# An S5 layer gated with a feed-forward layer on one core: a recurrence at every second token, one-pass silu, and a new order of the work

## The chip, the core and the metric

One core of a Trainium2 chip runs the program. The metric is device time in microseconds (us): the median of several executions of the compiled program. Most executions agree within 1.5% with the fastest of their kernel and are called fast here. A few were slower: some of the kernel before (up to 356.99 us against 349.31), one of e7 (352.45) and one of e10 (313.36, at a granted clock of 0.825 where the others had 0.85). A ratio compares fast runs alone. Where a run is compared with another, both were timed in the same rounds or set against the same kernel before (e9 to e12 ran on another chip than e1 to e8; the kernel before took 350.84 us there).

Engines in the profile: PE is TensorE's matmuls, PEld its weight loads, DVE is VectorE, ACT is ScalarE, POOL is GpSimd, SP is SyncE, which only issues DMAs here. A name with a small q (SPq, ACTq) is the sequencer of that engine. L345 is line 345 of the kernel that the profile is of, so the numbers differ from kernel to kernel.

## The reference, cut to what matters

```python
S, D, F = 2048, 448, 1792                     # tokens, model width, feed-forward width
g  = sigmoid((x * gate_w).sum(-1))            # one gate per token
dt = exp(log_dt); lam = exp(dt * Lambda)      # 448 complex lanes
B_bar = ((lam - 1) / Lambda)[:, None] * B
Bu = x @ B_bar.T                              # complex input
h_t = lam * h_{t-1} + Bu_t                    # 2048 steps, independent per lane
a  = 2 * real(h @ C.T) + x * Dskip
b  = silu(x @ w1) @ w2
out = g * a + (1 - g) * b                     # [1, 2048, 448] bf16
```

The recurrence over 2048 tokens is complex. Both kernels turn it into two real scans per lane: the input is rotated back by the lane's angle, `v_t = u_t * exp(-i*t*theta)`; then real and imaginary part each follow `g_t = r * g_{t-1} + v_t` with a real `r`, which is one scan instruction of VectorE; the result is rotated forward again. The rotations need a table of cosines and sines.

## The kernel before

A helper records every operation with the names of the buffers that it reads and writes, and turns these into semaphore waits. Each engine is given its own instructions as one list, in the order in which the program recorded them, and a wait in that list holds up what stands behind it.

The feed-forward tile. Silu takes two ScalarE passes and a VectorE product:

```python
def ffn1_tile(tc, fb):                        # 4 matmuls of 512 columns; the 4th uses 64 rows only
    T.op("pe", mm, reads=["w1", "xt"], writes=[f"ps{bank}"])
    T.op("act", ... activation(sig[slot], ps[:, bank, 0:512], AF.Sigmoid))            # L331
    T.op("act", ... activation(aT[:, fb, :], ps[:, bank, 0:512], AF.Copy))            # L342
    T.op("dve", ... tensor_tensor(aT[:, fb, :], aT[:, fb, :], sig[slot], ALU.mult))   # L345
```

The recurrence: 4 groups of lanes times 4 chunks of 512 tokens make 16 rounds.

```python
def s5_bu(pb, tc):                            # 2 x 4 matmuls, 2 evictions by ScalarE (L385)
    ...
def s5_rot_scan(pb, tc):                      # all VectorE
    p1 = ur*COS; p2 = ui*SIN; vr = p1+p2      # bf16, L398 to L402
    p1 = ui*COS; p2 = ur*SIN; vi = p1-p2      # bf16, L404 to L408
    ... carry in from the chunk before (4 small operations) ...
    gr = scan(R, vr); gi = scan(R, vi)        # float32 out, L437, L439
    q1 = gr*COS; q2 = gi*SIN; Hre = q1-q2     # L452 to L456
    q1 = gr*SIN; q2 = gi*COS; Him = q1+q2     # L458 to L462
```

The order, with feed-forward tiles strewn between the rounds, and the DMA names (all parts of x have one name, so that each DMA waits for the one before):

```python
for eb in range(4):
    T.dma("sp", ... dma_start_transpose(xt[eb][:, :], x2[:, c0:c0 + 128]), g_x, writes=["xt"])
... parameter arithmetic on 128 x 448 rows, B_bar on 4 x 128 x 448, tables; ffn1 tiles between ...
for step in range(4):
    for tcc in range(NTC):
        s5_bu(step, tcc)
        ... up to 7 ffn1 tiles or 2 ffn2 blocks ...
        s5_rot_scan(step, tcc)
for tb in range(12, 16): ffn2_block(tb)
for tb in range(NTB):    final_block(tb, tb)  # 8 matmuls, gate, one ACT pass, three DVE passes, store
```

## Time and profile before

| | before |
|---|---|
| time, median of 4 | 351.14 us (349.35 to 353.99) |
| span of the profiled run | 348.3 us |
| PE / DVE / ACT busy | 197.8 / 228.5 / 133.2 us |
| mean granted clock of TensorE | 0.794 |
| chain that ended last | DVE 54%, ACT 18%, PE 12%, DMA 9% |

The page of the kernel before. The first lines are busy time, share of the span and number of instructions of each engine; the rows of digits cut the span into 40 slices of 8.7 us, where a digit is the busy share in tenths, and PEclk is the granted clock of TensorE in tenths of full speed; the last line is the chain of waits followed back from the last instruction.

```profile
span 348.3 us, 2549 instructions
PE 197.8 (57%) x774; PEld 66.2 (19%) x784; DVE 228.5 (66%) x458; ACT 133.2 (38%) x258; POOL 1.6 (0%) x11
...
PE   0002722501760599810484995575994665899994
DVE  0000269981574699999675799484899484927776
PEclk9999955655555559985596999696999696899998
...
DVE 54%; ACT 18%; PE 12%; DMA 9%; issue 4%; ACTq 2%; DVEq 0%
```

No engine is full. The granted clock of TensorE is 0.50 in much of the time in which it has little to do (0.50 from 80 to 130 us) and 1.00 in the dense stretch from 310 to 340 us; in the first 40 us, in which TensorE is busy for 7.5 us only, the view lists 1.00. The windows view (busy time and count for each engine in a stretch, then granted clock, DMA share and GB/s) shows three stages: head, rounds, output.

```profile
33.00:116.00 83.00, 30.75 (x71) 6.54 (x72) 48.32 (x95) 43.10 (x74) 0.00 (x0) 0.59 0.15 38
116.00:296.00 180.00, 121.57 (x439) 39.51 (x448) 144.17 (x296) 69.31 (x129) 0.00 (x0) 0.81 0.00 1
296.00:348.00 52.00, 44.82 (x248) 19.55 (x248) 36.02 (x67) 18.33 (x53) 0.00 (x0) 0.94 0.22 65
```

The waits view (who waited for what: us in total, times, longest) and the groups by form (busy us, mean ns of one, idle time just before) of the kernel before:

```profile
DVE t L345 <- ACT t L342: 82.9, 40, 36.1
...
L331 ACT ACTIVATE t<-ps 128x512 bf16<-128x512 f32 x56 | 33.6, 599 | 93.1 <-DVE t L345 75.2 <-PE ps L325 17.9
L437 DVE TENSOR_TENSOR_SCAN t<-t 128x512 f32<-128x512 f32 x12 | 15.2, 1264 | 0.0
L452 DVE TENSOR_TENSOR t<-t 128x512 bf16<-128x512 f32 x12 | 8.0, 667 | 0.0
L404 DVE TENSOR_TENSOR t<-t 128x512 bf16<-128x512 bf16 x12 | 5.1, 425 | 0.4
```

The first line is the silu hand-over: VectorE stood 82.9 us in front of silu's product, 36.1 of it once at the start, when the first tile's inputs had not landed yet. The second is the other side: ScalarE stood 75.2 us in front of the sigmoid until VectorE had done a product, because VectorE came to it only after the scans that stood before it in its own order. One full-width round of rotations and scans costs VectorE 6 x 0.42 + 2 x 1.25 + 4 x 0.68 + 2 x 0.42 = 8.6 us.

### The profile page before, as it was taken

Reading aid. Unit: us, or ns where it says so; the run is one execution under the profiler, and the core shown is the slowest. Engines: PE = TensorE matmul, PEld = TensorE weight load, DVE = VectorE, ACT = ScalarE, POOL = GpSimd, SP = SyncE. Lnnn points to the kernel's source line nnn. Section 1 sums busy time; section 2 is a strip of 40 time slices with the busy share of each in tenths; the row PEclk is TensorE's granted clock in tenths of the full one; section 3 lists DMA queues with packets and bytes.
Section 4 is the critical chain, followed back from the end, with each engine's and each line's share of the span. In section 5 each row is a group of like instructions: output and inputs, shape, how many; then the busy total and the mean of one; then the engine's idle time right before and its main releaser. Section 6 shows DMA issues by size and latency. Waiting matters only on the chain.

```text
span 348.3 us, 2549 instructions
## 1 busy us (share of the span) xinstructions
PE 197.8 (57%) x774; PEld 66.2 (19%) x784; DVE 228.5 (66%) x458; ACT 133.2 (38%) x258; POOL 1.6 (0%) x11
## 2 busy tenths in 40 slices
PE   0002722501760599810484995575994665899994
PEld 0000100100110124300020441121441111444331
DVE  0000269981574699999675799484899484927776
ACT  0003880319624622400363433454432545124443
POOL 1000000000000000000000000000000000000000
PEclk9999955655555559985596999696999696899998
DMA  6877421100000100000000000000000000003332
GB/s 100 147 192 204 125 53 40 26 2 0 0 0 17 24 0 0 0 1 0 0 0 2 0 2 0 1 1 0 0 2 0 0 0 0 0 2 105 109 104 68
DMA packets 23661, 11.55 MB, mean 33 GB/s; under 512 B 16672, under 2 KB 23200, under 8 KB 23648
## 3 DMA queue, kind: packets, MB, share of 16 engines
q1 hardware_dynamic: 18304, 5.77, 7.2%
q10 hardware_dynamic: 5344, 5.62, 6.5%
q8 instruction: 6, 0.10, 0.1%
q14 instruction: 7, 0.06, 0.1%
HBM read 5.62 MB, written 1.84 MB: 21 GB/s over the span
## 4 chain that ended last, share of the span: by engine, by line
DVE 54%; ACT 18%; PE 12%; DMA 9%; issue 4%; ACTq 2%; DVEq 0%
PE ps L325 8%; DVE t L437 5%; DVE t L439 5%; DMA t<-in_B_w_dram 5%; ACT t L342 4%; PE ps L357 4%; DVE t L505 3%; DVE t L458 3%; ACT t L331 3%; DVE t L460 3%; DVE t L454 3%; DVE t L452 3%; DVE t L546 2%; ACT t L499 2%; DVE t L456 2%
## 5 line engine op out<-in xcount | busy, mean ns | idle before, releaser
L325 PE MATMUL ps<-t 128*128 128x512 bf16 (+1 forms) x218 | 77.9, 469 | 105.4 <-ACT t L342 81.0
L345 DVE TENSOR_TENSOR t<-t 128x512 bf16<-128x512 bf16 x56 | 23.1, 424 | 83.0 <-ACT t L342 82.9
L331 ACT ACTIVATE t<-ps 128x512 bf16<-128x512 f32 x56 | 33.6, 599 | 93.1 <-DVE t L345 75.2
L379 PE MATMUL ps<-t 128*128 128x512 bf16 (+1 forms) x124 | 42.8, 458 | 16.3 <-ACT t L385 15.7
L325 PEld LDWEIGHTS ps<-t 128*128 128x128 bf16 x224 | 18.9, 104 | 163.6 <-issue 143.8
L357 PE MATMUL ps<-t 128*128 128x448 bf16 x224 | 46.0, 366 | 1.6 <-DVE t L345 1.6
L342 ACT ACTIVATE t<-ps 128x512 bf16<-128x512 f32 x56 | 33.5, 598 | 0.0
L357 PEld LDWEIGHTS ps<-t 128*128 128x128 bf16 x224 | 22.1, 101 | 24.4 <-issue 3.6
L385 ACT ACTIVATE t<-ps 128x512 bf16<-128x512 f32 (+1 forms) x32 | 18.7, 602 | 16.5 <-PE ps L379 11.5
L476 PE MATMUL ps<-t 128*128 128x448 bf16 x64 | 22.8, 357 | 1.5 <-ACT t L499 1.5
L363 ACT ACTIVATE t<-ps 128x448 bf16<-128x448 f32 x16 | 8.7, 543 | 37.7 <-PE ps L357 37.7
L479 PE MATMUL ps<-t 128*128 128x448 bf16 x64 | 22.5, 352 | 0.0
L437 DVE TENSOR_TENSOR_SCAN t<-t 128x512 f32<-128x512 f32 (+1 forms) x16 | 20.2, 1265 | 0.0
L379 PEld LDWEIGHTS ps<-t 128*128 128x128 bf16 (+1 forms) x128 | 11.1, 103 | 47.8 <-issue 43.7
L439 DVE TENSOR_TENSOR_SCAN t<-t 128x512 f32<-128x512 f32 (+1 forms) x16 | 19.9, 1247 | 0.0
L505 DVE SCALAR_TENSOR_TENSOR t<-t 128x448 f32<-128x448 bf16 x16 | 10.9, 684 | 12.8 <-ACT t L499 12.2
L546 DVE TENSOR_TENSOR t<-t 128x448 f32<-128x448 f32 (+1 forms) x17 | 10.0, 617 | 5.3 <-ACT t L560 3.2
L538 ACT ACT_TABLE_LOAD x1 | 1.3, 1283 | 30.5 <-issue 30.5
L534 PE MATMUL ps<-t 1*128 1x1 bf16 x16 | 0.6, 161 | 20.6 <-DMA t<-in_gate_w_dram 20.6
L458 DVE TENSOR_TENSOR t<-t 128x512 bf16<-128x512 f32 (+1 forms) x16 | 11.1, 691 | 0.6
L508 DVE SCALAR_TENSOR_TENSOR t<-t 128x448 bf16<-128x448 bf16 x16 | 11.0, 685 | 0.6
L454 DVE TENSOR_TENSOR t<-t 128x512 bf16<-128x512 f32 (+1 forms) x16 | 11.0, 689 | 0.0
(88 smaller groups left out, 199.7 us busy)
## 6 DMA issues: line engine op xcount, KB each, us to landing
t<-in_A_x_dram ACTq DMA_DIRECT2D x16, 112.0 KB, 2.0
out_dram<-t SPq DMA_DIRECT2D x16, 112.0 KB, 1.8
t<-in_B_w_dram ACTq DMA_DIRECT2D x1, 1568.0 KB, 7.7
t<-in_B_w_dram ACTq DMA_DIRECT2D x3, 448.0 KB, 3.7
t<-in_B_w_dram ACTq DMA_DIRECT2D x1, 224.0 KB, 3.6
t<-in_A_log_dt_dram ACTq DMA_DIRECT2D x1, 112.0 KB, 3.9
t<-in_A_Lambda_re_dram ACTq DMA_DIRECT2D x1, 112.0 KB, 4.2
t<-in_A_Lambda_im_dram ACTq DMA_DIRECT2D x1, 112.0 KB, 4.4
```

What stands on the lines that cost most here:

```text
L325: ins = pe.matmul(ps[:, bank, 0:512], w1s[i][p0:p0 + K, fb * 128:(fb + 1) * 128], xt[i][p0:p0 + K, t0:t0 + 512], start=(i == 0), stop=(i = ...
L331: T.op("act", lambda eng: eng.activation(sig[slot][:, :], ps[:, bank, 0:512], AF.Sigmoid), reads=[f"ps{bank}"], writes=[f"sig{slot}"])
L342: T.op("act", lambda eng: eng.activation(aT[:, fb, :], ps[:, bank, 0:512], AF.Copy), reads=[f"ps{bank}"], writes=[f"aT{fb}"])
L345: lambda eng: eng.tensor_tensor(aT[:, fb, :], aT[:, fb, :], sig[slot][:, :], ALU.mult),
L357: ins = pe.matmul(ps[:, bank, 0:D_MOD], aT[:, fb, tl:tl + 128], w2s[:, fb, :], start=(fb == 0), stop=(fb == NFB - 1))
L379: ins = pe.matmul(ps[0:q0 + M, bank, 0:512], Bb[p0:p0 + K, i, lane0mm:lane0mm + q0 + M], xt[i][p0:p0 + K, t0:t0 + 512], start=(i == 0), st ...
L437: T.op("dve", lambda eng: eng.tensor_tensor_scan(gr[q0:q0 + M, :], Rbc, vr[q0:q0 + M, :], init_r, ALU.mult, ALU.add), reads=[f"vr{s}", "cf ...
L439: T.op("dve", lambda eng: eng.tensor_tensor_scan(gi[q0:q0 + M, :], Rbc, vi[q0:q0 + M, :], init_i, ALU.mult, ALU.add), reads=[f"vi{s}", "cf ...
L454: T.op(Epool, lambda eng: eng.tensor_tensor(qp2[q0:q0 + M, :], gi[q0:q0 + M, :], SIN, ALU.mult), reads=[f"gi{s}", f"SIN{pb}"], writes=[nqp2])
L458: T.op(Edve, lambda eng: eng.tensor_tensor(qd1[q0:q0 + M, :], gr[q0:q0 + M, :], SIN, ALU.mult), reads=[f"gr{s}", f"SIN{pb}"], writes=[nqd1])
L476: ins = pe.matmul(ps[:, bank, 0:D_MOD], Hre[q0:q0 + M, pb, t0:t0 + 128], C2T[q0:q0 + M, pb, :], start=first, stop=False)
L479: ins = pe.matmul(ps[:, bank, 0:D_MOD], Him[q0:q0 + M, pb, t0:t0 + 128], Ci2T[q0:q0 + M, pb, :], start=False, stop=(pb == 3))
```

## The change

The intent is to halve the sequential work and to take everything that is not a matmul off the long chain.

- **Recurrence at every second token.** With `h_{2k+1} = lam^2 * h_{2k-1} + (lam*B x_{2k} + B x_{2k+1})` only odd states are scanned: 1024 steps. The input matmul takes two tokens at once (7 blocks of 128 rows). An even token's output is `C lam h_{2k-1} + (C B + D) x_{2k}`, where the dense `K0 = C B + D` is built once and costs four matmuls per tile.
- **Scaling in C.** The factor `(lam-1)/Lambda` goes into C, so raw B is transposed and parameters are 128 x 4 columns rather than 128 x 448 rows. Real and imaginary part of the last 64 lanes share one full tile.
- **Silu in one ScalarE pass**; the gate on VectorE with an accumulating product; only DMA transposes; separate names for separate DMAs; tables of 1024 steps.
- **A new order.** All "side" work (tables, C, gate) is pumped between the first 28 feed-forward tiles; then input matmuls and scans, then the rest of the feed-forward layer, then the output tiles.

The diff, cut to its core (the whole replaces most of the file; cuts are marked `...`):

```diff
-            T.op("act", lambda eng: eng.activation(sig[slot][:, :], ps[:, bank, 0:512], AF.Sigmoid), ...)
-                T.op("act", lambda eng: eng.activation(aT[:, fb, :], ps[:, bank, 0:512], AF.Copy), ...)
-                     lambda eng: eng.tensor_tensor(aT[:, fb, :], aT[:, fb, :], sig[slot][:, :], ALU.mult),
+            T.op("act", lambda e: e.activation(a[:, fb, :], ps[:, bank, :], AF.Silu), ...)
...
+        def bu(m, h):                            # m: real/imaginary tile, h: half of the 1024 pairs
+                for j in range(7):
+                    ins = pe.matmul(ps[:, bank, :], LT[:, m, j, :], XT[:, j, h * 512:(h + 1) * 512], ...)
+            T.op("act", lambda e: e.activation(HS[:, m, 8 + h * 512:8 + (h + 1) * 512], ps[:, bank, :], AF.Copy), ...)
...
-            T.op("dve", lambda eng: eng.tensor_tensor_scan(gr[q0:q0 + M, :], Rbc, vr[q0:q0 + M, :], init_r, ...
+                T.op("dve", lambda e: e.tensor_tensor_scan(G[:, c, :], rb, Q1[:, c, :], 0.0, ...   # 1024 long
...
+        def ytile(kt, odd):
+                for m in range(8):
+                    ins = pe.matmul(ps[:, bank, 0:D], HS[:, m, o0:o0 + 128], C[:, m, :], ...)
+                ... odd: 4 small diagonal matmuls; even: 4 x matmul(XT[:, j], KT[:, j, :]) ...
+            T.op("dve", ... scalar_tensor_tensor(o, ps[:, bank, 0:D], GT[:, 1, tile:tile + 1], bs(tile), ...
...
+        side = chain(side_params(), side_tables(0), side_coef(), side_diag(), side_C(True),
+                     side_tables(1), side_gate(), side_tables(2), side_tables(3), side_C(False))
+        for _ in range(2):
+            next(side)
+        for c in range(2):
+            for fb in range(NFB):
+                ffn1(c, fb)
+                pump()
+        for pt in range(3):
+            ... bu(2*pt, h), bu(2*pt+1, h), pump(2) ...; scan(pt) ...
+        ... bu(6, h), bu(7, h); rest of side; scan(3); k0; ffn2(0); ffn1(2); ffn2(1); ffn1(3); ffn2(2) ...
+        for q in range(4):
+            ffn2(3, q); ytile(q, 0); ytile(q, 1); store(q)      # then the last eight tiles
```

## The prediction

> **What bounds the kernel now.** No single engine: PE 57% busy, DVE 66%, ACT 38% (page, part 1), but the chain that ended last is 54% DVE, 18% ACT, 12% PE, 9% DMA. Three stages show in the windows view. (1) 0–116 us: input DMAs wait for each other (chain: log_dt, Lambda_re, Lambda_im, Dskip, then w1 until 32.9 us), then parameter arithmetic on 128x448 rows (0.62 us an op, reciprocal 2.95) and cos/sin tables. (2) 116–296 us: 16 rotate-and-scan rounds, DVE 97% busy in them; one costs 6x0.42 + 2x1.25 + 4x0.68 + 2x0.42 = 8.6 us; between rounds DVE stands behind the silu hand-over (PE, two ACT passes, one DVE multiply per tile). (3) 296–348 us: one ffn2 group and 16 output tiles at 2.2 us, paced by DVE/ACT; full TensorE clock.
>
> **What changes.** Scan length halves. Sizes of 1024 estimated from the 512 durations (bf16 product 0.42 to 0.69, scan 1.25 to 2.3, float product 0.68 to 1.22): three pairs at 15.1 us plus 6.9 us for the packed last one, 52 us of DVE for 138. Silu becomes one ACT pass with no DVE multiply (56x0.60 ACT and 56x0.42 DVE gone). ACT u-evictions fall from 32 to 16. Output tiles need no ACT, one DVE op. Row arithmetic becomes 128x4 (0.16 us an op). PE hardly shrinks: matmuls of 512 columns go from 352 to 336, of about 448 from 352 to about 400. K=64 pieces vanish. Added on DVE ahead of the first scan: B combinations (7), C combinations (16) at about 1.05 us (0.39 + 0.68), four tables at 2.7, coefficients 5, 16 gate products at 0.68.
>
> **Where the critical path goes.** From the instruction order:
> - About 17–20 us: inputs (transposes no longer serialised) and parameters; then DVE runs all side work in order. It also gates ACT: silu tiles sit behind table and tanh instructions in ACT's order, so the first 28 ffn1 tiles are paced by DVE. B combinations to 25, table 0 to 28, coefficients/diagonals 34, odd C 43, table 1 46, gate about 62 (two buffers, reloads about 2 us each), tables 2 and 3 share a buffer with ACT, 77; last silus to about 83 us. TensorE is sparse here and at half clock (0.50 in such windows now).
> - Then PE never waits for the scans (they end about 146 us, the output tiles start about 185). Its remaining order, at the cadence of dense full-clock stretches (0.19 us per 448; 0.215 per 512 estimated by columns): input matmuls 24, K0 6, ffn2 43, ffn1 24, output tiles 33 = 130 us, plus 4 for warm-up and boundaries. Last eviction and store 3 us.
>
> Span about 83+134+3 = 220; the measured time stands 3 us above the span: **223 us**, range 206 to 243. Chances: faster by over 2% 0.98, same 0.01, slower 0.01.
>
> The Trainium skill ("TensorE: Matmul & The Clock Gate", What's actually happening) says the array clock is halved until activity lasts some microseconds; this trace agrees (0.50 in sparse windows, 1.00 at 310–340 us). It matters twice: the DVE-paced head stays slow, the tail runs full.
>
> **What would show it.** Right: PE over 90% busy at clock near 1.0 in the last 60%, chain nearly all PE there; first 80 us DVE-led with PE under 5 tenths; scans ending some 40 us before the first output tile; DVE total near 135–150 us, ACT near 85. Wrong: PE waiting on scans; output tiles paced by evictions through two banks; ACT over 100.
>
> **What would make it wrong.** Transposes from on-chip memory, or about 12 MB of input at the 160–200 GB/s seen early, delaying the gate loads past 50 us (slower by 5–20); table loads of 1.28 us at every silu/sine switch; a cheaper gate phase (faster by up to 10); reduced clock or slower weight loads at odd offsets in the dense tail.

## The result, and the profile after

| | before | after |
|---|---|---|
| time, median of 4 | 351.14 us | 215.06 us (214.43 to 217.03) |
| ratio of the fast runs | | 0.6131 (0.608 to 0.6182) |
| span of the profiled run | 348.3 us | 213.8 us |
| PE / DVE / ACT busy | 197.8 / 228.5 / 133.2 us | 163.9 / 114.1 / 71.3 us |
| chain that ended last | DVE 54%, ACT 18%, PE 12% | PE 62%, DVE 15%, DMA 11% |

A ratio here sets the fast runs of one kernel against those of the other in the same rounds, so it isn't quite the ratio of the medians quoted. Forecast 223 (range 206 to 243), measured 215.06. The page after:

```profile
span 213.8 us, 2064 instructions
PE 163.9 (77%) x784; PEld 77.2 (36%) x792; DVE 114.1 (53%) x212; ACT 71.3 (33%) x112; POOL 7.3 (3%) x16
...
PE   0550009939703349999999999999999999999994
DVE  0439999903567696499999999700000021213332
PEclk9997556975985557999999999999999999999999
...
PE 62%; DVE 15%; DMA 11%; SPq 7%; ACT 3%; issue 1%; DVEq 0%
```

A slice is 5.3 us here. PE is at 9 from the sixteenth slice on, the clock from the seventeenth: one dense stretch. The windows view cuts it at the end of the head (82 us) and at the end of the scans (138 us):

```profile
14.00:82.00 68.00, 30.03 (x97) 11.17 (x99) 49.79 (x128) 29.22 (x42) 0.00 (x0) 0.68 0.54 133
82.00:138.00 56.00, 55.79 (x268) 26.54 (x271) 50.62 (x51) 23.13 (x40) 0.00 (x0) 0.99 0.00 1
138.00:211.00 73.00, 72.56 (x398) 37.49 (x398) 10.55 (x16) 15.60 (x26) 0.00 (x0) 1.00 0.06 23
```

TensorE is busy 128.4 of 129 us after the head. In the head it is busy 30 of 68 us. The waits view says what it stood for, and the chain (start, us, what) says what stood behind that:

```profile
PE ps L493 <- ACT AT L498: 37.9, 5, 17.6
...
DVE JK L457 <- DMA OT<-in_A_x_dram: 11.9, 5, 8.3
```

```profile
41.92 9.41 DMA OT<-in_A_x_dram
51.35 0.65 DVE JK L457 x2
...
75.27 0.95 ACT G L384
76.25 1.15 ACT COS L385
77.39 0.49 ACT AT L498
77.89 0.05 issue
77.93 3.59 PE ps L493 x8
81.53 7.12 PE ps L528 x29
```

L498 is silu. In these long waits it did not wait for its own matmuls: it stood in ScalarE's order behind tables (L382 to L385) and the tanh from which the gate's sigmoid is made, which wait for VectorE, which for 8.3 us waited for the first gate tile. Two groups by form answer to those of before, the scan and the product with a float32 operand, now on 1024 elements:

```profile
L564 DVE TENSOR_TENSOR_SCAN G<-P,Q 128x1024 f32<-128x1024 f32 x7 | 15.7, 2278 | 0.0
L561 DVE TENSOR_TENSOR Q<-G,COS 128x1024 bf16<-128x1024 f32 x6 | 7.3, 1210 | 0.0
L561 DVE TENSOR_TENSOR Q<-HS,COS 128x1024 bf16<-128x1024 bf16 x7 | 4.8, 685 | 3.9 <-ACT HS L532 3.9
```

The scan and the float32 product nearly double from 512 to 1024 elements (1264 to 2278 ns, 667 to 1210 ns), and the bf16 product goes from 425 to 685 ns.

So the change turned a kernel in which VectorE and ScalarE pass work to and fro for most of 348 us into a head of 82 us with the same disease, and a tail of 129 us that is nothing but matmuls. That raises the question that the experiments answer: which parts of the change earned the 136 us?

### The profile page after: what moved, and what is told of

Its sections match the earlier page's. It is cut to its first block, busy times and chain, and to the rows that moved or that the text cites. A ratio compares the mean times of both kernels' runs of the same rounds, so it can differ in the third digit from the quotient of the medians.

```text
span 213.8 us, 2064 instructions
## 1 busy us (share of the span) xinstructions
PE 163.9 (77%) x784; PEld 77.2 (36%) x792; DVE 114.1 (53%) x212; ACT 71.3 (33%) x112; POOL 7.3 (3%) x16
## 4 chain that ended last, share of the span: by engine, by line
PE 62%; DVE 15%; DMA 11%; SPq 7%; ACT 3%; issue 1%; DVEq 0%
PE ps L511 20%; PE ps L493 13%; PE ps L528 12%; PE ps L610 11%; DMA OT<-in_A_x_dram 8%; SPq L208 4%; SPq L205 3%; DVE JK L457 3%; PE ps L621 3%; DMA Y<-in_A_B_re_dram 3%; PE ps L543 3%; DVE TMP L340 2%; DVE BB L342 2%; DVE G L380 2%; ACT COS L385 1%
## 5 line engine op out<-in xcount | busy, mean ns | idle before, releaser
L493 PE MATMUL ps<-XT,W1E 128*128 128x512 bf16 x110 | 34.8, 482 | 38.5 <-ACT AT L498 37.9
L511 PE MATMUL ps<-W,AT 128*128 128x448 bf16 x224 | 43.4, 352 | 0.0
L498 ACT ACTIVATE AT<-ps 128x512 bf16<-128x512 f32 x56 | 32.4, 596 | 15.6 <-PE ps L493 15.6
L493 PEld LDWEIGHTS ps<-XT,W1E 128*128 128x128 bf16 x112 | 12.5, 117 | 59.9 <-ACT AT L498 42.0
L511 PEld LDWEIGHTS ps<-W,AT 128*128 128x128 bf16 x224 | 21.7, 98 | 20.0 <-issue 0.2
L528 PE MATMUL ps<-XT,LT 128*128 128x512 bf16 x110 | 25.1, 389 | 0.1
L493 PE MATMUL ps<-XT,W1O 128*128 128x512 bf16 x108 | 24.0, 379 | 0.2
L457 DVE SCALAR_TENSOR_TENSOR JK<-OT,GWB 128x448 bf16<-128x448 bf16 x16 | 10.0, 625 | 12.5 <-DMA OT<-in_A_x_dram 11.9
L564 DVE TENSOR_TENSOR_SCAN G<-P,Q 128x1024 f32<-128x1024 f32 x7 | 15.7, 2278 | 0.0
L610 PE MATMUL ps<-CE,HS 128*128 128x448 bf16 x64 | 13.4, 352 | 0.0
L610 PE MATMUL ps<-CO,HS 128*128 128x448 bf16 x64 | 13.4, 352 | 0.0
L382 ACT ACTIVATE SIN<-G 128x1024 bf16<-128x1024 f32 x4 | 4.2, 1056 | 22.4 <-DVE G L380 22.4
```

Of the source, the lines that this page charges most:

```text
L457: T.op("dve", lambda e, s=s, i=i, kt=kt: e.scalar_tensor_tensor(JK[:, :], OT[s][:, i * D:(i + 1) * D], 1.0, GWB[:, i * D:(i + 1) * D], ALU ...
L493: ins = pe.matmul(ps[:, bank, :], W[:, j, fb * 128:(fb + 1) * 128], XT[:, j0 + j, h * 512:(h + 1) * 512], start=(j == 0), stop=(j == 3))
L498: T.op("act", lambda e: e.activation(a[:, fb, :], ps[:, bank, :], AF.Silu), reads=[f"ps{bank}"], writes=[f"AT{c % 2}_{fb}"])
L511: ins = pe.matmul(ps[:, bank, 0:D], a[:, fb, q * 128:(q + 1) * 128], W2[:, fb, :], start=(fb == 0), stop=(fb == NFB - 1))
L528: ins = pe.matmul(ps[:, bank, :], LT[:, m, j, :], XT[:, j, h * 512:(h + 1) * 512], start=(j == 0), stop=(j == 6))
L564: T.op("dve", lambda e: e.tensor_tensor_scan(G[:, c, :], rb, Q1[:, c, :], 0.0, ALU.mult, ALU.add), reads=[f"Q1{c}", "rr"], writes=[f"G{c}"])
```

## The experiments

The theories. **Theory 1:** after the head TensorE bounds the kernel, and the scans have 33 us to spare (they end at 137.9 us, the first output tile starts at 170.9 us). So in this program the halved recurrence, the headline of the change, is worth far less than its 50 us of VectorE work. **Theory 2:** the head is set by the order of instructions on ScalarE and VectorE and by what that order waits for. **Theory 3:** in the kernel before, the silu hand-over cost much more than its busy time. Rivals are named in each expectation.

### Slack of the scans: once 22 us more, once 52 us more

```diff
-        def scan(pt):
+        def scan(pt, junk=False):               # junk: results go to a scratch tile, not to HS
...
-            for _ in scan(pt):
+            for _ in chain(scan(pt, True), scan(pt)):     # e1: groups 0 and 3 only; e2: all four
                 pass
```

> The changed kernel with the rotate-and-scan of lane groups 0 and 3 done twice (first pass into a scratch tile, result stays right): about 22 us more VectorE work. In the profile of the changed kernel the scans end at 137.9 us and the first output tile starts on TensorE at 170.9 us, so there are 33 us of slack. Theory 1 (the scans are off the critical path, TensorE bounds everything after 81 us): 215 us, within 1 us of the changed kernel, scans ending about 160 us. Rival (VectorE still bounds, the busy TensorE only looks so): about 237 us, or some in-between value.

> All four rotate-and-scan passes done twice, result right: 50 to 52 us more VectorE work, which is what a scan over every token (twice the length) would cost VectorE in this schedule. Theory 1: the scans end about 188 us instead of 137.9, 17 us after TensorE would need them, so about 232 us (+17), with one TensorE wait of about 17 us before the first output tile, perhaps a half-clock start after it. Rival (scans bound the kernel): +50, 265 us. Rival (scans never matter): 215.

| run | time, us | ratio to before | result |
|---|---|---|---|
| changed kernel | 215.06 | 0.6131 | right |
| e1, +22 us of scans | 216.3 (215.56 to 217.39) | 0.615 (0.6097 to 0.6203) | right |
| e2, all scans twice | 234.59 (233.05 to 235.12) | 0.666 (0.6604 to 0.6717) | right |

In e1 VectorE is busy 134.7 us instead of 114.1, and the time hardly moves: 1.2 us by the medians, 0.7 by the ratios, and the intervals overlap. The last two scan lines of VectorE and the first output matmuls of TensorE in its trace:

```profile
156.45 1.22 DVE L561 TENSOR_TENSOR HS<-G,COS 128x1024 bf16<-128x1024 f32 x1
157.60 1.22 DVE L561 TENSOR_TENSOR HS<-G,SIN 128x1024 bf16<-128x1024 f32 x1
...
170.77 1.68 PE L610 MATMUL ps<-CE,HS 128*128 128x448 bf16 x8
```

In e2 the scans end at 186.1 us and TensorE waits for them once, where it never did before:

```profile
PE ps L610 <- DVE HS L561: 16.4, 1, 16.4
```

Theory 1 gave +17; 19.5 were measured. In the profiled run, the fastest of the four, the span is 17.5 us longer: 15.4 because the first output tile starts later, and about 2 because the clock is low around the wait (0.50 from 180 to 186 us, 0.64 from 186 to 192). So in this schedule, halving the scan is worth 18 to 20 us, not 50 and not 136.

### The tail: half of the second feed-forward matmul

```diff
-                for fb in range(NFB):
+                for fb in range(7):
                     ins = pe.matmul(ps[:, bank, 0:D], a[:, fb, q * 128:(q + 1) * 128], W2[:, fb, :],
-                                    start=(fb == 0), stop=(fb == NFB - 1))
+                                    start=(fb == 0), stop=(fb == 6))
```

> The changed kernel with only 7 of the 14 accumulation steps of the second feed-forward matmul (result wrong on purpose): 112 matmuls of 448 columns fewer. Theory 1 (TensorE-bound tail): 112 x 0.19 = 21 us faster, 194 us; the scans (end 137.9) would still be in time for the output tiles (150). Rival (tail paced by evictions through two banks, or by VectorE): less than 8 us faster.

Measured 194.16 us (193.85 to 195.05), ratio 0.5527. The comparison with the reference uses a tolerance that this cut stays within; it is wrong on purpose all the same. Against 215.06 that is 20.9 us for 112 matmuls, 0.187 us each. The tail is TensorE's, matmul by matmul.

### The head: gate loads first

```diff
-        ld("sp", W2[:, :, :], ..., "W2")
-        ld("sp", W1O[64:128, 0, :], ..., "W1Oa")
-        ld("sp", W1O[:, 1:4, :], ..., "W1Ob")
         ... gate weights ...
         for c in range(2):
             for fb in range(NFB):
                 ffn1(c, fb)
                 pump()                           # the gate tiles are loaded in here
+        ld("sp", W2 ...); ld("sp", W1O ...); ld("sp", W1O ...)
```

> The changed kernel with the W2 and odd-token W1 loads (3.1 MB) issued behind the gate loads instead of ahead of them. VectorE stood 8.3 us (43.1 to 51.35) for the first gate load, and that wait is in the chain. Theory 2 (the head until 81 us is one chain through VectorE's program order, so a wait on it counts in full): 7 to 9 us faster, 206 to 208 us. Rival (the wait only moves: other gate waits, or W2 now late for TensorE): less than 3 us faster.

Measured 208.57 us (207.48 to 209.86), ratio 0.593: 6.5 us faster than the changed kernel. VectorE's waits for gate tiles fell from 11.9 to 4.7 us in the trace, the input matmuls start at 76.4 us instead of 81.5, and nothing came back later. It is a little under the 7 to 9 expected. VectorE no longer waited for the first gate tile at all, but it started on B 2.3 us later in that run (16.97 instead of 14.67 us), mainly because B landed later, so the gate began 6.0 us earlier (45.35 instead of 51.35) and not 8.3.

### The head: ScalarE's order alone

```diff
-        ... ffn1 tiles with pump() between, then bu and scan by group ...
+        for c in range(2):
+            for fb in range(NFB):
+                ffn1(c, fb)
+        ... side work up to odd C; all 16 bu; rest of the side work; the four scans ...
```

> The changed kernel with only the program order of its first part changed: all 28 first-half feed-forward tiles and then all 16 input-matmul evictions stand ahead of the later table, tanh and gate work in ScalarE's order; VectorE does the same work in nearly the same order (gate still waits for its load). Theory 2 (TensorE idles 38 us in the head because ScalarE's in-order queue holds silu behind tables and tanh that wait for VectorE): TensorE finishes these tiles at about 40 us instead of 81, is then held by the second part of the tables on ScalarE until about 78 us for its K0 evictions, and later waits for the scans, which now end about 138 us on VectorE: about 184 us in all. Rival (the head is bound by data arriving, or by the half clock): 205 us or more.

Measured 188.55 us (186.44 to 189.16), ratio 0.5381: 26.5 us faster with the same operations, and 4.5 slower than the 184 expected. TensorE finished the 28 tiles at 35.4 us instead of 81.5 (about 40 expected), and the input matmuls at 61. Then it stood behind ScalarE once more:

```profile
PE ps L543 <- ACT KT L550: 14.9, 1, 14.9
```

These are the K0 evictions behind tables 2 and 3. One step of my expectation was wrong: there was no wait for scans at all. They end at 133.9 us and the first output tile starts at 141.7.

### In the kernel before: silu alone

```diff
-            T.op("act", ... activation(sig[slot][:, :], ps[:, bank, 0:512], AF.Sigmoid), ...)
-                T.op("act", ... activation(aT[:, fb, :], ps[:, bank, 0:512], AF.Copy), ...)
-                     lambda eng: eng.tensor_tensor(aT[:, fb, :], aT[:, fb, :], sig[slot][:, :], ALU.mult), ...
+            T.op("act", lambda eng: eng.activation(aT[:, fb, :], ps[:, bank, 0:512], AF.Silu), ...)
```

> The kernel before with one change: silu in one ScalarE pass instead of sigmoid, copy and a VectorE product. Removes 56 x 0.42 = 23 us of VectorE and 33 us of ScalarE work and the waits of VectorE between scan rounds. Theory 3 (in the kernel before, silu stands in the way of the scan rounds, so its waits count too): rounds shrink to 16 x 8.6 = 138 us from 180, head loses about 5: 40 to 48 us faster, about 305 us. Rival (only VectorE's busy time counts): 23 us faster, 328.

Measured 283.03 us (281.08 to 285.03), ratio 0.8068. The expectation was too small: 68 us faster by the fast runs (the 70 of later expectations has slow runs of the kernel before in it), not 40 to 48. The spans of the profiled runs split it. Up to the first rotation: 116.7 us before, 98.5 here, 18 less. From there to the last one: 189.3 before, 140.1 here, 49 less. After it: 42.3 and 40.6. My term for the rounds (42) was about right, the term for the head (5) was too small by 13. In the head, silu's passes also stood between the parameter steps, and two table loads fewer precede the first rotation (9 instead of 11, 1.28 us each); no run separates these. The rounds before and here (the third pair after the length is DVE):

```profile
116.66:306.00 189.34, 130.61 (x478) 43.85 (x488) 152.96 (x314) 70.18 (x129) 0.00 (x0) 0.81 0.00 1
...
98.47:238.53 140.06, 123.21 (x495) 43.81 (x504) 135.80 (x272) 52.43 (x90) 0.00 (x0) 0.91 0.00 1
```

VectorE's work in the rounds fell by 17 us, its idle time there by 32 (from 36.4 to 4.3): that is what Theory 3 says. VectorE has no room left now. One edit of three lines earns, by itself, half of what the whole change earned.

### In the changed kernel: silu undone

```diff
+            sl = fb % 2
-            T.op("act", lambda e: e.activation(a[:, fb, :], ps[:, bank, :], AF.Silu), ...)
+            T.op("act", lambda e: e.activation(SIG[sl][:, :], ps[:, bank, :], AF.Sigmoid), ...)
+            T.op("act", lambda e: e.activation(a[:, fb, :], ps[:, bank, :], AF.Copy), ...)
+            T.op("dve", lambda e: e.tensor_tensor(a[:, fb, :], a[:, fb, :], SIG[sl][:, :], ALU.mult), ...)
```

> The changed kernel with one part of the change undone: silu as in the kernel before (sigmoid, copy, VectorE product). Adds 56 x 0.6 us of ScalarE and 56 x 0.42 us of VectorE work. Theory (what silu costs depends on what it stands in front of): in the tail two ScalarE passes of 0.6 us exceed TensorE's 0.86 us per tile, so 28 x 0.34 = 10 us more; in the head ScalarE and VectorE get 17 and 12 us more and table loads of 1.28 us at each change between sigmoid and sine, of which 10 to 20 us count: 235 to 245 us, a loss of 20 to 30. Rival (silu is worth the same 70 us here as in the kernel before): 285.

Measured 243.54 us (242.55 to 244.06), ratio 0.6942: 28.5 us slower, inside the expected range. It was run on another chip. The same part that is worth 68 us in the old program is worth 28.5 us in the new one. About 14 us lie in the head: the first input matmul starts that much later than in the changed kernel. In the tail the loss took partly another form than I had argued: the products stand behind the last scans in VectorE's order, and TensorE waits for them once.

```profile
153.92 6.42 PE L494 MATMUL ps<-XT,W1O 128*128 128x512 bf16 x19 [11.95 <-ACT AT L502]
```

Table loads of ScalarE rise from 3 to 9, at 1.283 us each. The Trainium skill, page "ScalarE: Activation LUTs", section "Table sets: the hidden batching unit", advises to batch activation calls by set, not by function. The traces agree in kind: silu, sine, tanh, copy and absolute value alternate all through the changed kernel after one load at the first silu, and in e9 a load stands at each change between sigmoid and sine.

### In the kernel before: DMAs that do not wait for each other

```diff
-                xt[eb][:, :], x2[:, c0:c0 + 128]), g_x, writes=["xt"])
+                xt[eb][:, :], x2[:, c0:c0 + 128]), g_x, writes=[T.part("xt")])   # own name; readers wait for all
...  the same for B, C, w1 and the parameter rows ...
```

> The kernel before with one change: the parts of x, B, C, w1 and the parameter rows get separate names in the dependency bookkeeping, so that their DMAs no longer wait for each other. First feed-forward matmul at about 15 us instead of 32.9. Theory: the head is one chain, so 15 to 20 us faster, about 333 us. Rival (bandwidth bound: loads in parallel finish no sooner): less than 5 us faster.

Measured 347.48 us (343.11 to 352.45), ratio 0.9852 with an interval of 0.9492 to 1.0212, so the times alone establish no difference (the fast runs are 4.8 us apart, but the interval holds both nothing and the 15 us at the lower end of the theory). The trace decides: the first feed-forward matmul came at 30.7 us instead of 32.9, not at 15, so the theory's first step failed, and a gain of less than 5 us is what the rival said. That matmul waited for x:

```profile
30.74 2.52 PE L336 MATMUL ps<-t 128*128 128x512 bf16 x5 [19.01 <-DMA t<-in_A_x_dram]
```

The DMA view shows how late loads land (last number: median us from issue to landing); first before, then this run:

```profile
t<-in_B_w_dram ACTq DMA_DIRECT2D x1, 1568.0 KB, 7.7
...
t<-in_A_x_dram SPq DMA_TRANSPOSE x4, 4.8
```

```profile
t<-in_B_w_dram ACTq DMA_DIRECT2D x1, 1568.0 KB, 20.3
...
t<-in_A_x_dram SPq DMA_TRANSPOSE x4, 11.2
```

In the first 40 us the DMA engines are busy 89% of the time instead of 73%, but move only 170 GB/s instead of 161: with all loads running together, the large ones land later. The four transposes of x, which are needed first, were also issued late: SyncE took 7.1 us (median) to issue one, instead of 2.3, and started the last at 23.9 us. Whether w1, w2 (not needed for another 80 us) or the transposes themselves held them up was not separated. The Trainium skill, page "DMA: Bandwidth & Descriptors", section "Issuing engines are not separate DMA queues", states that DMAs issued from different engines run on the same 16 DMA engines and interleave; this run agrees, with the 4.8 us of SyncE's transposes that became 11.2 when ScalarE had issued all its loads in the first 7.7 us (though the transposes no longer wait for each other either).

### In the kernel before: half of the rounds

```diff
-                s5_rot_scan(pb, tcc)
+                if tcc % 2 == 0:
+                    s5_rot_scan(pb, tcc)
...  carry in from two chunks before; the output tiles read the neighbouring chunk ...
```

> The kernel before with every second rotate-and-scan round left out (result wrong on purpose; the output reads the neighbouring chunk instead), all else kept: the VectorE price of a recurrence at every second token, put into the old program. Removes 8 x 8.6 = 69 us of VectorE work. Theory (with the old silu the rounds also wait for its hand-over, and TensorE needs about 105 us for the work of the rounds): about 45 us faster, 306. Rival A (VectorE bounds): 69 us faster, 284. Rival B (scan length hardly matters): under 20.

> The same cut of every second round in the kernel before with single-pass silu (283 us; result wrong on purpose). There VectorE is busy 97% in the rounds, 139 us. Theory: the rounds fall to what TensorE needs for them, about 105 us at full clock, so about 35 us faster, 248 us. Rival (VectorE only): 69 us faster, 214, which would be the whole rest of the way to the changed kernel.

| run | time, us | ratio to before | against |
|---|---|---|---|
| e10, before, half of the rounds | 305.47 (fast runs 304.13 to 306.21, one slow 313.36) | 0.8703 (0.8654 to 0.8752) | 350.84 before: 45 faster |
| e11, the same with one-pass silu | 260.44 (258.91 to 261.62) | 0.7428 (0.7385 to 0.7472) | 283.03 of e6: about 23 faster |

Both results are wrong on purpose (relative error 0.051). e10's time came out as expected, in part by luck, since the 105 us stood in that expectation too and were too few. e11 was expected at 248, and the step that failed is the size of TensorE's work in the rounds: from the first round on TensorE is full for some 120 us rather than my 105: it is busy 118.1 us from 100 to 220. One of the six windows of 20 us (first pair after the length):

```profile
120.00:140.00 20.00, 19.80 (x75) 5.68 (x74) 13.03 (x25) 11.21 (x19) 0.00 (x0) 1.00 0.00 1
```

A tile of four 512-column matmuls takes 1.09 us there at full clock, and 0.86 us in the changed kernel (14 tiles in the 12.03 us from 122.92 on). The two tiles differ in the fourth matmul, on 64 rows instead of 128. The output tiles of before show it by starts:

```profile
310.19 0.35 PE L479 MATMUL ps<-t 128*128 128x448 bf16 x1
310.47 0.36 PE L476 MATMUL ps<-t 64*128 64x448 bf16 x1
310.67 0.35 PE L479 MATMUL ps<-t 64*128 64x448 bf16 x1
310.95 0.33 PE L490 MATMUL ps<-t 128*128 128x1 bf16 x4
```

Starts are 0.19 us apart among 128-row matmuls and 0.20 between the two with 64 rows, but 0.28 us on going to 64 rows and 0.28 on coming back. In the same stretch the weight load of a 128-row matmul starts with the matmul before it (at 310.00 for the one at 310.19), but at these two changes it starts only with its own matmul (310.47 and 310.95). No run isolates this by itself, so it is a likely cause of the 1.09 us and not a shown one.

### A better order

The theories say what a better kernel would be: the operations of the changed kernel, with silu and input evictions never behind side work in ScalarE's order, each scan as soon as its inputs are there, gate tiles loaded early through three buffers, and tables 2 and 3 between the scans.

```diff
+        all_ffn1(0);  run(side_params(), side_tables(0));  all_ffn1(1)
+        run(side_coef(), side_diag(), side_C(True))
+        pair(0);  run(side_tables(1));  pair(1); pair(2); pair(3)      # pair: the 4 bu of a group
+        run(scan(0));  k0(0..3);  run(side_gate(), side_tables(2));  all_ffn2(0)
+        run(scan(1));  all_ffn1(2);  run(side_tables(3));  all_ffn2(1)
+        run(scan(2));  all_ffn1(3);  run(side_C(False), scan(3));  all_ffn2(2)
+        ... output tiles as before ...
```

> The changed kernel with its work reordered to the theory: feed-forward tiles and input matmuls not behind tables, tanh or gate in ScalarE's order, gate inputs loaded early through three buffers, each scan as soon as its inputs are there, tables 2 and 3 between the scans. Theory 1 and 2 together: TensorE starts about 12 us and is then dense; 26 + 129 + start + tail gives 172 to 178 us, TensorE over 90% busy from 15 us on, scans ending about 125 us. Rival (something else, such as clock, DMA or bank waits, appears in its place): 190 us or more.

> The reordered kernel (178 us) with all four rotate-and-scan passes done twice (result right), so 52 us more VectorE work, as a scan over every token would need. In the reordered kernel the scans end at 126.7 us and the output tiles start at 133.5: only 7 us of slack are left instead of 33. Theory: the scans end at about 173 to 179, output tiles and last stores take 43 more: 216 to 223 us, 38 to 45 us slower, against 19 in the unreordered schedule. Rival (same price as there): 197.

| run | time, us | ratio to before | result |
|---|---|---|---|
| e8, reordered | 178.02 (177.22 to 178.58) | 0.5072 (0.5022 to 0.5123) | right |
| e12, reordered, all scans twice | 219.92 (219.49 to 220.1) | 0.6273 (0.6249 to 0.6297) | right |

Both came out as expected (e8 at the upper end of 172 to 178). The page of e8:

```profile
span 176.4 us, 2057 instructions
PE 158.9 (90%) x784; PEld 76.3 (43%) x792; DVE 114.0 (65%) x212; ACT 71.2 (40%) x112; POOL 7.3 (4%) x16
...
PE   0179996999979999959999999999999999999992
```

The engines do the same work as in the changed kernel, 37 us sooner, and the head's window shows it:

```profile
14.00:82.00 68.00, 62.83 (x282) 28.32 (x285) 61.36 (x133) 36.97 (x58) 0.00 (x0) 0.98 0.59 135
```

TensorE is busy 62.8 of these 68 us rather than 30.0. And with the slack gone (scans end at 126.7 us, output tiles start at 133.5), doubling the scans costs 42 us rather than 19.5.

```profile
PE ps L518 <- ACT LT L523: 21.8, 2, 16.1
...
PE ps L617 <- DVE HS L568: 14.4, 1, 14.4
```

The first of the two lines is the gate, now late because it stands behind the doubled first scans in VectorE's order; the second is the output tile waiting for the last scan. So a part of the 42 us is again the order.

## Why the prediction was right

It was 223 us; 215.06 were measured. The mechanism is confirmed at each step, with these sizes:

- **"DVE runs all side work in order. It also gates ACT"**: right. TensorE's waits of 37.9 us are on silu behind tables, and e5 removes 26.5 us of the time by order alone. Predicted end of the tables 77, measured 77.4; predicted end of the head 83, measured 81.5.
- **"Gate about 62"**: the gate started at 51.35 instead of 46 us, because its loads stood behind 3.1 MB of weights. This is the first cause in the list of what could go wrong. It was hidden in the total since the steps before it were some 3 us earlier than predicted and I had put 16 us on the gate products, which took 14.3 (51.35 to 65.7), and 15 on tables 2 and 3, which took 11.7. So the 77.4 us that met the 77 are in part luck: errors of opposite sign cancelled. e4 gives 6.5 us of the wait for the gate back.
- **"PE never waits for the scans"**: right, with 33 us of slack where I had 39 (146 and 185); e1 and e2 bracket it.
- **"130 us, plus 4 for warm-up and boundaries"**: measured 129.2 us from 81.5 to 210.7, all included. The extra 4 us did not appear: the first 29 input matmuls already ran at 0.25 us each (granted clock 0.86 from 82 to 86 us, 1.00 after that), with feed-forward tiles just before them. e3 confirms the price per matmul: 0.187 us against the 0.19 used. The Trainium skill, page "TensorE: Matmul & The Clock Gate", section "What's actually happening", describes a clock that is halved by default and released by sustained activity. From 20 us on the trace agrees: 0.50 from 20 to 30 us, when TensorE did nothing, 0.68 on average from 14 to 82 us, 0.99 to 1.00 after it. It doesn't fit that the view lists 1.00 for the first 14 us, in which TensorE was busy for 5.5 us only.
- **The 8 us of difference** are 1.5 in the head, about 4.8 in the tail and 1.3 in the step from span to time (1.7 in place of 3).
- **The sums for the busy times were wrong.** I wrote 135 to 150 us for VectorE and 85 for ScalarE; 114.1 and 71.3 were measured. My own terms for VectorE (52 + 24 + 11 + 5 + 11 + 11, the last for the 16 output operations) add up to 114. The total in the text was carelessly added, and since VectorE was not on the path it cost nothing.
- **"TensorE is sparse here"** was right on average but not in shape: in the head it works in bursts (slices of 9, then 0 to 3) as ScalarE frees its four banks, not under 5 tenths throughout.
- **"Table loads of 1.28 us at every silu/sine switch"** did not happen: 3 loads in all, against 11 before.

What the prediction did not say at all is what each part is worth. Taken alone: silu 68 us in the old program and 28.5 in the new; half of the scan work (69 us of VectorE's time in the old program, about 50 in the new) 45 us in the old, about 23 in the old with one-pass silu, 19.5 in the new, 42 in the reordered. These do not add up, and need not: each is read in a program in which something else waits next. Both together bring the kernel before to 260 us. What lies between that and 215 (parameters as columns instead of rows, full 128-row matmuls, output tiles with one pass, the order) was not taken apart further. Estimated from 0.23 us for each of the 56 + 32 tiles of four matmuls, the 64-row pieces alone are about 20 us of TensorE time.

## What to carry to other kernels

Before halving the work of an engine, find out whether anything waits for it: here three lines of silu are worth more than half of the scan work in the old program (68 against 45 us) and in the new one (28.5 against 19.5), because the silu sat where two engines handed work to each other, each in its own order. When an engine idles, look at what stands before the awaited instruction in the releasing engine's order, not only at the releaser: reordering the same operations took this kernel from 215 to 178 us. And the value of a part is not a constant of that part; measure it again when the rest has moved.

## What the Trainium skill lacked or had wrong

- "ScalarE: Activation LUTs", section "Table sets: the hidden batching unit", lists example sets but not where silu and sine are. The runs show that sine, tanh, copy and absolute value need no load once the table of silu is there (3 loads in 112 instructions of ScalarE, the last at the first silu), and that sigmoid and sine do (9 loads after going back to sigmoid).
- "ScalarE: Activation LUTs", section "What ACT_TABLE_LOAD costs", gives about 1283 ns for a load, which every trace here has, and adds a drain of about 1380 ns for each switch. That drain doesn't show here: in the changed kernel the cosine pass ends at 29.71 us, the load runs from 29.73 for 1.28 us, and silu starts at 31.02.
- "VectorE: DVE Perf Modes", section "The perf-mode tier table (the rule you actually need)", has no row for the scan; the skill's remark on the scan's speed stands on another page ("DVE: opcode table, instruction layouts, handler registers and perf-mode slots") and gives no time. Measured 1264 ns on 512 and 2278 ns on 1024 float32 elements, so 1.98 ns for each further element, against 1.06 for a product with a float32 operand (667 to 1210 ns).
- "DMA: Bandwidth & Descriptors", section "DMA Transpose (X-bar)", doesn't say what a transpose loses beside other transfers: 4.8 us from issue to landing became 11.2 us when the transposes of x no longer waited for each other and the weight and parameter loads were in flight with them. No run tells the two apart.
- "TensorE: Matmul & The Clock Gate", section "Why this matters for your kernels", says that a single matmul with 32 rows takes the time of one with 128. The two 64-row matmuls of an output tile of the kernel before agree (0.20 us from start to start, against 0.19), but each change between 128 and 64 rows (the upper half of the array) took 0.28 us. No run isolates it.
